# Attention and feed-forward kernel: float32 scores in the first six blocks, one output buffer per token group, three new plan estimates

## The chip, the cores and the metric

The kernel runs on one core of a Trainium2 chip as one launch. The core has a matrix engine (PE, with its weight loads shown apart as PEld), a vector engine (DVE), a scalar engine (ACT), a third one (POOL) and a queue that issues transfers (SP). The metric is the time on the device in microseconds (us); lower is better.

## The reference

Attention over 4 batches, 8 heads, 768 positions and 64 channels, then a feed-forward layer over the 3072 tokens that it gives.

```python
scores = scale * np.matmul(q, k.transpose(0, 1, 3, 2))
rel = pos[:, None] - pos[None, :]
is_global = pos[None, :] < int(n_global)          # 8 keys
is_local = (rel >= 0) & (rel < int(n_local))      # 96 keys
keep = is_global | is_local
dist = np.where(is_global & ~is_local, float(n_local), np.abs(rel))
scores = np.where(keep, scores - slopes * dist, -1000000000.0)
a = np.exp(scores - max); a = a / (sum + 1e-09)
x = matmul(a, v)                                  # (B, H, S, D) -> (B*S, H*D)
h = x @ w_in                                      # 512 -> 2048
g = h * (1.0 / (1.0 + np.exp(-h)))
return (g @ w_out).astype(np.float32)             # 2048 -> 512
```

## The kernel before, in words

**Tiling.** The 24 blocks (4 batches by 6) hold 128 tokens each; a block has 4 head pairs. A block looks at 128 keys if it is the first of its batch (NJ = 6 blocks per batch) and at 232 otherwise: 96 of the block before, 8 global ones and its own 128. Two blocks are a group for the feed-forward layer (12 groups of 256 tokens, 16 chunks f of the hidden width).

**A head pair's way.** PE turns keys and queries (`turn`, L448), ACT copies the high parts out of the PSUM bank (`high`, L503), and in blocks 0 to 5 DVE subtracts them to get the low parts (`low`, L507); both are float32r tiles, KH, KL, QH and QL. POOL carries the last 96 and the global keys over from the block before (`carry`, L514 and L516). `scores` (L528) adds three products, QH by KH, QH by KL and QL by KH, each for the two heads of the pair on partitions 0 to 63 and 64 to 127: six matmuls. DVE adds the bias and takes the extreme (L545), ACT takes the exponential (L553), PE turns the result (L578), ACT moves it to SBUF (L584), PE multiplies by the values (`values_q`, L612, in blocks 0 to 5, operands float32). After the fourth pair DVE divides the whole block (L628, tile xq), PE turns it back (L634), ACT and DVE make xh and xl (L643, L646). Blocks 6 to 23 use another form, with both parts stacked over the 128 partitions (`stack_scores`, L500; values at L598); the change leaves it as it is.

**Feed-forward.** `moe_h` (L763) takes 12 matmuls a chunk, `moe_o` (L788) 6. Groups 0 and 1 run side by side, since the weights come in one chunk after another: SP loads them, DVE puts each together from 64-bit words in three steps (L368, L374, L380), ACT makes the high part (L387), DVE the low part (L391). `moe_end` writes a group's two output tiles (`osb`), and `moe_out` sends each.

**What sets the order.** Nothing is ordered at run time. A planner (`Plan.run`) simulates the engines with costs in ns written at each `op(...)`, lets each engine take the ready operation of the lowest rank, and writes down the order; the engines then run their lists in that order and wait by semaphores. The estimate of a transfer is PAR["DL"] = 1900. Where the plan has PE without work before its time 60000 (PAR["WEND"]), it puts in a filler, a matmul of zeros that nothing reads (L899, tile wx), which keeps the engine at work. `big` is a pool of three buffers of 4 KB per partition: staged weights (w), R of the stacked blocks, weights that are read again for a check (c, L411), and the output tiles (osb) take turns in it.

```python
if best is None:
    if eng == "PE" and filler and t < fill_until and self.banks:
        order.append(lambda b=self.banks[-1]: filler(b))
```

Of the kernel before, what the change touches and what calls it, by code (L numbers as in the profile page):

```python
# [21 lines left out]
P = 128  # L22
# [5 lines left out]
FAR = 1.0e9  # L28
PAR = dict(

    LAT=140, SD=125, DL=1900, MG=60, T2=45000, LAT2=230, MG2=400, F0=600, F1=1200, C1=900, C2=3400, COLD=7000, WEND=60000,

    CAP=dict(po=4, av=2, s=4, h=3, tp=2, tq=4), HU=13,

# [136 lines left out]
def attn_moe(ctx, tc, q, k, v, n_global, n_local, w_in, w_out, out):  # L171
# [8 lines left out]
    NB = 2  # L180
# [213 lines left out]
    for n in range(2 * NFC):  # L394
        rank = PAR["C0"] + PAR["CR"] * n
        a, m, x = [] if lent(n) is not None else [Buf("big")], Buf("mid"), lent(n)
        o = op("DMA", 1456, rank - PAR["LW"], (lambda n=n: stage(n, "w")), [o_l[x]] if not a else (), a, PAR["DL"])
        o = op("DVE", 335, rank, (lambda n=n: conv1(n)), [o], [*a, m])
        o = op("DVE", 602, rank, (lambda n=n: conv2(n)), [o], [*a, m])
        o = op("DVE", 602, rank, (lambda n=n: conv3(n)), [o], [*a, m])  # L400
        if x is not None:
            o_l[x] = o
        o_wf = o
        hi = op("ACT", 520, rank, (lambda n=n: conv_hi(n)), [o] + (o_l if n >= 2 * NFC - 4 else []), [m])
        lo = op("DVE", 602, rank, (lambda n=n: conv_lo(n)), [hi], [m])
        o_w.append((hi, lo))
# [38 lines left out]
    def turn(i, nm, tp, p0=0, p1=NHP):  # L445
        blk[i]["t", nm, p0] = ps = bank(tp, NHP, P)
        for hp in range(p0, p1):
            nc.tensor.transpose(ps[:, hp], blk[i][nm][:, 2 * hp:2 * hp + 2, :], ident)  # L448

    def part(i, x):  # L450
        if x not in blk[i]:
            blk[i][x] = sb2.tile([P, NHP, WIN if x[0] == "K" else P], F32R, name=x)
        return blk[i][x][:, :, C1:] if x[0] == "K" else blk[i][x]


# [46 lines left out]
    def high(i, nm, p0=0, p1=NHP):  # L502
        nc.scalar.copy(part(i, nm.upper() + "H")[:, p0:p1], blk[i]["t", nm, p0][:, p0:p1])  # L503

    def low(i, nm, p0=0, p1=NHP):
        hi, lo = (part(i, nm.upper() + x)[:, p0:p1] for x in "HL")
        nc.vector.tensor_sub(lo, blk[i]["t", nm, p0][:, p0:p1], hi.bitcast(F32))  # L507

    def carry(i, x, glob):
        part(i, x)  # L510
        new, old = blk[i][x], blk[i - 1][x].bitcast(F32)
# [9 lines left out]
    def scores(i, hp, s):  # L521
        t = blk[i]
        w0, n = cols(i)
        t["s", hp] = ps = [bank(x, WIN) for x in s]
        for m, (x, y) in enumerate((("QH", "KH"), ("QH", "KL"), ("QL", "KH"))):
            for a in range(2):
                r = slice(a * D, (a + 1) * D)
                nc.tensor.matmul(  # L528
                    ps[a][:, :n], t[x][r, hp], t[y][r, hp, w0:], start=m == 0, stop=m == 2
                )  # L530

    def top_of(i, hp, a):
        t = blk[i]
# [120 lines left out]
    for i in range(B * NJ):  # L654
# [3 lines left out]
        if not i:  # L658
            xn = dict(k=Buf("qkn"), q=Buf("qkn"))
            for p0 in (0, NHP // 2):  # L660
                for nm in "kq":
                    p1, tp = p0 + NHP // 2, Buf("tq")
                    hi, lo = kk[nm.upper() + "H"], kk[nm.upper() + "L"]
                    o = op("DMA", 728, rank - lr, (lambda nm=nm, a=2 * p0, b=2 * p1: load(0, nm, a, b)), (), [xn[nm]], PAR["DL"])
                    o = op("PE", 220, rank, (lambda nm=nm, tp=tp, a=p0, b=p1: turn(0, nm, tp, a, b)), [o], [xn[nm], tp, hi, lo])
                    ob[nm + "h", p0] = o = op("ACT", 264, rank, (lambda nm=nm, a=p0, b=p1: high(0, nm, a, b)), [o], [tp, hi])
                    ob[nm + "l", p0] = op("DVE", 331, rank, (lambda nm=nm, a=p0, b=p1: low(0, nm, a, b)), [o], [tp, hi, lo])
        for nm in "kq" if i else "":
            xn, tp = Buf("qkn"), Buf("tq")
            hi, lo = kk[nm.upper() + "H"], kk[nm.upper() + "L"]  # L670
            o = op("DMA", 1456, rank - lr, (lambda i=i, nm=nm: load(i, nm)), (), [xn], PAR["DL"])
            o = op("PE", 440, rank, (lambda i=i, nm=nm, tp=tp: turn(i, nm, tp)), [o], [xn, tp, hi, lo])
            if i >= PAR["I0"]:
                hs = [op("ACT", 478, rank, (lambda i=i, nm=nm, a=a: stack_high(i, nm, a, False)), [o], [tp, x])
                      for a, x in enumerate((hi, lo))]
                for a, x in enumerate((hi, lo)):
                    y = x if nm == "k" else kk["R"]
                    ob[nm, a] = op("DVE", 602, rank, (lambda i=i, nm=nm, a=a: stack_low(i, nm, a)),
                                   hs + ([o_wf] if nm == "q" else []), [tp, x, y])
                    if nm == "q":  # L680
                        ob[nm, a, 2] = op(
                            "ACT", 520, rank + PAR["RQ"], (lambda i=i, a=a: twin_low(i, a)), [ob[nm, a]], [y]
                        )
                        ob[nm, a, 1] = op(
                            PAR["QS"], dict(ACT=520, POOL=1930, DVE=335)[PAR["QS"]], rank + PAR["RQ"],
                            (lambda i=i, nm=nm, a=a: stack_high(i, nm, a, True)), [hs[a]], [x]
                        )
                continue
            ob[nm + "h"] = op("ACT", 478, rank, (lambda i=i, nm=nm: high(i, nm)), [o], [tp, hi])
            ob[nm + "l"] = op("DVE", 602, rank, (lambda i=i, nm=nm: low(i, nm)), [ob[nm + "h"]], [tp, hi, lo])  # L690
        if j:
            old = o_k[i - 1]
            stacked = i >= PAR["I0"]
            for x, y in ((("KH", ("k", 0)), ("KL", ("k", 1))) if stacked else (("KH", "kh"), ("KL", "kl"))):
                for gl, cost in ((True, 227), (False, 1400)):
                    ob[x, gl] = op(
                        "POOL", cost, rank, (lambda i=i, x=x, gl=gl: carry(i, x, gl)),
                        [*(old[z] for z in (((y, 0), (y, NHP // 2)) if i == 1 else (y,))), old.get((x, True)), ob[y]],
                        [kb[i - 1][x], kk[x]],
                    )  # L700
# [5 lines left out]
        for hp in range(NHP):  # L706
            u = NHP * i + hp
            stacked = i >= PAR["I0"]
            s, pe, pt, tp = [Buf("s") for _ in range(1 if stacked else 2)], Buf("pe"), Buf("pt"), Buf("tp")
            ks = [kk[x] for x in ("KH", "KL", "QH", "QL") + (("R",) if stacked else ())]  # L710
# [23 lines left out]
            before["move"] = o_m[-1]  # L734
            pts.append(pt)
            if not plain:
                last = op("PE", 460 if j else 230, u - PAR["RV"], (lambda i=i, hp=hp, av=pav: values_q(i, hp, av)),
                          [o_m.pop(), last] + o_v, [pt, pav, kk["vn"]] + ([kk["vp"]] if j else []))
            elif not stacked or hp == NHP - 1:
                last = op("PE", ((1860 if j else 980) if stacked else 540 if j else 290), u - PAR["RV"],  # L740
                          (lambda i=i, hp=hp, av=pav: values_of(i, hp, av)),
                          [*o_m, last] + o_v, [*pts, pav, xb[g]["xh"], xb[g]["xl"], kk["vn"]] + ([kk["vp"]] if j else []))
                o_m, pts = [], []
# [46 lines left out]
            )  # L790

    def moe_end(g, tt, half=None):
        if ("out", g, tt) not in mo:
            mo["out", g, tt] = sb3.tile([P, DM], F32, name="osb", tag="big")
        h = slice(0, DM) if half is None else slice(half * DM // 2, (half + 1) * DM // 2)
        o, po = mo["out", g, tt][:, h], mo["po", g, tt][:, h]
        if tt % 2 and not half:
            nc.scalar.mul(o, po, 0.5)
        else:
            nc.vector.tensor_scalar(o, po, 0.5, None, ALU.mult)  # L800

    def moe_out(g, tt, half=None):
        n = g * NB + tt
        h = slice(0, DM) if half is None else slice(half * DM // 2, (half + 1) * DM // 2)
        eng = nc.scalar if half == 0 else nc.sync
        eng.dma_start(out[n * P:(n + 1) * P, h], mo["out", g, tt][:, h])

    o_h = {}
    FIRST = -1e6
    for g in range(NGRP):  # L810
# [3 lines left out]
        for f in range(NFC):  # L814
# [260 lines left out]
```

## Time and profile before

| | |
|---|---|
| median of 3 runs | 734.85 us (733.05 to 736.74) |
| the profiled execution | 735.96 us |
| its span, first to last instruction | 734.2 us |
| PE busy | 722.7 us (98%), 5236 matmuls |
| DVE, ACT, POOL busy | 471.3, 422.0, 28.1 us |
| mean granted PE clock | 0.996 |

The busy time of PE is a union of matmuls whose ends are modelled, so they overlap; what a matmul takes from the engine is read from the distance between the starts of neighbours. The span falls into four stretches: a start of some 8 us; the attention of blocks 0 to 3 up to some 60 us; feed-forward groups 0 and 1 up to some 153 us, with the remaining heads of blocks 4 and 5 and the first of block 6 up to some 167 us; and from there ten groups of the same pattern to the end.

### The profile page before, as it was taken

Reading aid. Unit: us, or ns where it says so; the run is one execution under the profiler, and the core shown is the slowest. Engines: PE = TensorE matmul, PEld = TensorE weight load, DVE = VectorE, ACT = ScalarE, POOL = GpSimd, SP = SyncE. Lnnn points to the kernel's source line nnn. Section 1 sums busy time; section 2 is a strip of 40 time slices with the busy share of each in tenths; the row PEclk is TensorE's granted clock in tenths of the full one; section 3 lists DMA queues with packets and bytes.
Section 4 is the critical chain, followed back from the end, with each engine's and each line's share of the span. In section 5 each row is a group of like instructions: output and inputs, shape, how many; then the busy total and the mean of one; then the engine's idle time right before and its main releaser. Section 6 shows DMA issues by size and latency. Waiting matters only on the chain.

```text
span 734.2 us, 14157 instructions
## 1 busy us (share of the span) xinstructions
PE 722.7 (98%) x5236; PEld 650.9 (89%) x5236; DVE 471.3 (64%) x1417; ACT 422.0 (57%) x1105; POOL 28.1 (4%) x91
## 2 busy tenths in 40 slices
PE   8999999999999999999999999999999999999996
PEld 6889988988999999898999999999899999998995
DVE  4689999986567566666665665765666756544322
ACT  5887544477566466565665665755756756543321
POOL 2010000000000000000000000000000000000000
PEclk9999999999999999999999999999999999999999
DMA  7587553424033242241340421512412312000001
GB/s 153 137 255 194 166 172 107 152 82 115 26 105 87 55 112 68 74 113 45 87 111 16 128 73 41 142 53 61 130 44 70 103 54 56 30 1 1 29 0 34
DMA packets 117500, 63.97 MB, mean 87 GB/s; under 512 B 93744, under 2 KB 110384, under 8 KB 117424
## 3 DMA queue, kind: packets, MB, share of 16 engines
q1 hardware_dynamic: 116992, 62.86, 31.6%
q8 instruction: 43, 0.70, 0.4%
q14 instruction: 33, 0.27, 0.1%
q10 hardware_dynamic: 432, 0.13, 0.1%
HBM read 56.69 MB, written 6.29 MB: 86 GB/s over the span
## 4 chain that ended last, share of the span: by engine, by line
PE 97%; DMA 1%; DVE 1%; issue 0%; SPq 0%; ACT 0%; DVEq 0%
PE bank L763 38%; PE bank L788 36%; PE bank L578 5%; PE bank L598 4%; PE bank L500 4%; PE bank L448 3%; PE bank L612 3%; PE bank L528 2%; PE bank L899 1%; DMA qn<-in_q_dram 1%; DMA out_dram<-osb 1%; PE bank L634 0%; DVE osb L800 0%; DVE R L487 0%; DVE pe L569 0%
## 5 line engine op out<-in xcount | busy, mean ns | idle before, releaser
L763 PE MATMUL bank<-xh,WIH 128*128 128x256 f32 x768 | 224.6, 292 | 0.8 <-ACT xh L643 0.8
L763 PE MATMUL bank<-xl,WIH 128*128 128x256 f32 x768 | 217.0, 283 | 0.7 <-DVE xl L646 0.7
L763 PE MATMUL bank<-xh,WIL 128*128 128x256 f32 x768 | 215.6, 281 | 0.0
L763 PEld LDWEIGHTS bank<-xh,WIH 128*128 128x128 f32 x768 | 145.2, 189 | 10.0 <-issue 2.2
L763 PEld LDWEIGHTS bank<-xl,WIH 128*128 128x128 f32 x768 | 145.4, 189 | 7.3 <-DVE xl L646 0.9
L763 PEld LDWEIGHTS bank<-xh,WIL 128*128 128x128 f32 x768 | 145.6, 190 | 0.0
L788 PE MATMUL bank<-WOH,gh 128*128 128x512 f32 x336 | 136.1, 405 | 0.0
L769 ACT ACTIVATE th<-bank 128x256 f32<-128x256 f32 x192 | 73.6, 383 | 106.6 <-PE bank L763 104.6
L788 PE MATMUL bank<-WOH,gl 128*128 128x512 f32 x336 | 132.4, 394 | 0.0
L788 PE MATMUL bank<-WOL,gh 128*128 128x512 f32 x336 | 131.9, 393 | 0.0
L777 ACT CAST gh<-th 128x256 fp32r<-128x256 f32 x192 | 77.4, 403 | 91.9 <-PE bank L788 62.4
L773 DVE SCALAR_TENSOR_TENSOR th<-th,bank 128x256 f32<-128x256 f32 x192 | 80.4, 419 | 64.8 <-ACT th L769 63.3
L781 DVE TENSOR_TENSOR gl<-th,gh 128x256 fp32r<-128x256 f32 x192 | 81.5, 424 | 50.7 <-ACT gh L777 48.6
L545 DVE CUSTOM_DVE_ANT_0 pe<-bank,B 128x232 f32<-128x232 f32 (+1 forms) x192 | 69.0, 376 | 63.2 <-PE bank L500 57.2
L553 ACT ACTIVATE pe<-pe,NM 128x232 f32<-128x232 f32 (+1 forms) x192 | 90.3, 471 | 18.6 <-DVE NM L545 16.4
L584 ACT COPY pt<-bank 128x512 f32<-128x512 f32 (+1 forms) x96 | 52.6, 549 | 52.5 <-PE bank L578 52.3
L788 PEld LDWEIGHTS bank<-WOH,gl 128*128 128x128 f32 x336 | 63.0, 188 | 15.1
L788 PEld LDWEIGHTS bank<-WOH,gh 128*128 128x128 f32 x336 | 63.4, 189 | 6.7 <-issue 0.3
L788 PEld LDWEIGHTS bank<-WOL,gh 128*128 128x128 f32 x336 | 63.4, 189 | 6.4
L578 PE MATMUL bank<-ident,pe 128*128 128x128 f32 (+1 forms) x352 | 55.0, 275 | 0.1
L578 PEld LDWEIGHTS bank<-ident,pe 128*128 128x128 f32 (+1 forms) x352 | 42.0, 137 | 6.6 <-DVE pe L569 0.6
L411 DVE TENSOR_REDUCE TOP<-c 128x1 f32<-128x512 int16 x64 | 42.3, 681 | 3.2 <-DMA c<-in_moe_w_in_dram 3.2
(119 smaller groups left out, 939.1 us busy)
## 6 DMA issues: line engine op xcount, KB each, us to landing
c<-in_moe_w_in_dram SPq DMA_DIRECT2D x16, 512.0 KB, 4.0
c<-in_moe_w_out_dram SPq DMA_DIRECT2D x16, 512.0 KB, 4.4
vn<-in_v_dram SPq DMA_DIRECT2D x24, 256.0 KB, 3.4
w<-in_moe_w_in_dram SPq DMA_DIRECT2D x12, 512.0 KB, 3.8
w<-in_moe_w_out_dram SPq DMA_DIRECT2D x12, 512.0 KB, 3.6
kn<-in_k_dram SPq DMA_DIRECT2D x23, 256.0 KB, 3.0
qn<-in_q_dram SPq DMA_DIRECT2D x23, 256.0 KB, 3.1
out_dram<-osb SPq DMA_DIRECT2D x23, 256.0 KB, 3.0
```

The source lines that it names most:

```text
L411: nc.vector.tensor_reduce(TOP[:, i, n:n + 1], top, AX.X, (ALU.min, ALU.max)[i], apply_absolute_value=True)
L500: nc.tensor.matmul(ps[:, a, :n], t[x][:, hp], t[K[a]][:, hp, w0:], start=not m, stop=m == 1)
L545: nc.vector.tensor_tensor_reduce(t["p", hp][:, a, :n], t["s", hp][a][:, :n], B1[:, h] if i % NJ else B0[:, h], -SC, 3.0e38, ALU.add, ALU.m ...
L553: nc.scalar.activation(x, x, AF.Exp, bias=NM[:, i * H + h:i * H + h + 1], scale=-1.0, accum_out=t["sum", hp][:, a:a + 1],)
L578: nc.tensor.transpose(ps[:n, c, a], pe[:, a, c0:c0 + n], ident)
L584: nc.scalar.copy(t["pt", hp][:, c], t["tp", hp][:, c])
L763: nc.tensor.matmul(ph, w[:, c, fs], x[:, c], start=not c and not n, stop=c == NCC - 1 and n == 2)
L769: nc.scalar.activation(th, mo["ph", g, f], AF.Tanh, scale=0.5)
L773: nc.vector.scalar_tensor_tensor(gf, gf, 1.0, mo["ph", g, f], ALU.add, ALU.mult)
L777: nc.scalar.copy(gh, mo["th", g, f])
L781: nc.vector.tensor_sub(gl, mo["th", g, f], mo["gh", g, f].bitcast(F32))
L788: nc.tensor.matmul(po, a[:, s], w_o(w, f), start=f == 0 and n == 0, stop=f == NFC - 1 and n == 2)
```

## The change

1. `part` makes the key and query tiles of blocks 0 to 5 float32 (names KHw and QHw). `low`, KL and QL are gone there. `scores` is one float32 product for each of the two heads: two matmuls in the program instead of six.
2. `carry` moves only the high tile in blocks 1 to 5; the plan's costs of a carry go from 227 and 1400 to 155 and 455.
3. The plan's cost of `values_q` goes from 460 to 900 (230 to 450 in a batch's first block). The cost of scores stays 640. (The third cost that the diff changes, in the branch of `values_of`, is not used: IV = I0 = 6.)
4. The plan's estimate for a weight transfer is 2900 and for an output transfer 3400, both 1900 before.
5. A group's two output tiles are one tile of 4 KB in one `big` buffer.

```diff
@@ PAR
-    LAT=140, SD=125, DL=1900, MG=60, ...
+    LAT=140, SD=125, DL=1900, DW=2900, DO=3400, MG=60, ...
@@ weights
-        o = op("DMA", 1456, rank - PAR["LW"], (lambda n=n: stage(n, "w")), [o_l[x]] if not a else (), a, PAR["DL"])
+        o = op("DMA", 1456, rank - PAR["LW"], (lambda n=n: stage(n, "w")), [o_l[x]] if not a else (), a, PAR["DW"])
@@ part
+    def whole(i):
+        return i < PAR["I0"]
+
     def part(i, x):
         if x not in blk[i]:
-            blk[i][x] = sb2.tile([P, NHP, WIN if x[0] == "K" else P], F32R, name=x)
+            f = whole(i)
+            blk[i][x] = sb2.tile(
+                [P, NHP, WIN if x[0] == "K" else P], F32 if f else F32R, name=x + "w" * f, tag=x
+            )
@@ low, carry, scores
-    def low(i, nm, p0=0, p1=NHP):
-        hi, lo = (part(i, nm.upper() + x)[:, p0:p1] for x in "HL")
-        nc.vector.tensor_sub(lo, blk[i]["t", nm, p0][:, p0:p1], hi.bitcast(F32))
...
-        for m, (x, y) in enumerate((("QH", "KH"), ("QH", "KL"), ("QL", "KH"))):
-            for a in range(2):
-                r = slice(a * D, (a + 1) * D)
-                nc.tensor.matmul(
-                    ps[a][:, :n], t[x][r, hp], t[y][r, hp, w0:], start=m == 0, stop=m == 2
-                )
+        for a in range(2):
+            r = slice(a * D, (a + 1) * D)
+            nc.tensor.matmul(ps[a][:, :n], t["QH"][r, hp], t["KH"][r, hp, w0:], start=True, stop=True)
@@ the operations of a block
-                    ob[nm + "l", p0] = op("DVE", 331, rank, (lambda nm=nm, a=p0, b=p1: low(0, nm, a, b)), [o], [tp, hi, lo])
-            ob[nm + "l"] = op("DVE", 602, rank, (lambda i=i, nm=nm: low(i, nm)), [ob[nm + "h"]], [tp, hi, lo])
-            for x, y in ((("KH", ("k", 0)), ("KL", ("k", 1))) if stacked else (("KH", "kh"), ("KL", "kl"))):
-                for gl, cost in ((True, 227), (False, 1400)):
+            for x, y in ((("KH", ("k", 0)), ("KL", ("k", 1))) if stacked else (("KH", "kh"),)):
+                for gl, cost in ((True, 155), (False, 455)):
-                last = op("PE", 460 if j else 230, u - PAR["RV"], (lambda i=i, hp=hp, av=pav: values_q(i, hp, av)),
+                last = op("PE", 900 if j else 450, u - PAR["RV"], (lambda i=i, hp=hp, av=pav: values_q(i, hp, av)),
@@ output
-        if ("out", g, tt) not in mo:
-            mo["out", g, tt] = sb3.tile([P, DM], F32, name="osb", tag="big")
+        if ("out", g) not in mo:
+            mo["out", g] = sb3.tile([P, NB, DM], F32, name="osb", tag="big")
...
+        ob = Buf("big")
         for tt in range(NB):
-            ob = Buf("big")
...
-                op("DMA", 728, FIRST + rank, (lambda g=g, tt=tt, h=h: moe_out(g, tt, h)), [o], [ob], PAR["DL"])
+                op("DMA", 728, FIRST + rank, (lambda g=g, tt=tt, h=h: moe_out(g, tt, h)), [o], [ob], PAR["DO"])
```

Since the plan is made anew, the order changes too, up to the start of group 2; from there on all engines have the same order as before. PE's list holds 74 fillers before and 28 after, ten of them at its very start in both; 144 score matmuls before and 48 after. DVE's list loses the 14 subtractions of `low`, POOL's ten carries.

**Place 1: PE at the start**, from the turning of the second half of block 0's keys (kn) on; qn are the queries, KH, KL, QH and QL the split tiles, KHw and QHw the float32 ones, wx the filler's zeros. Before:

```order
L448 MATMUL bank_84<-ident,kn 128x128 x2
L899 LDWEIGHTS wx
L899 MATMUL bank_82<-wx 128x256
L448 MATMUL bank_85<-ident,qn 128x128 x2
L528 MATMUL bank_86<-KH,QH 128x128
L528 MATMUL bank_87<-KH,QH 128x128
L528 MATMUL bank_86<-KL,QH 128x128
L528 MATMUL bank_87<-KL,QH 128x128
L528 MATMUL bank_86<-KH,QL 128x128
L528 MATMUL bank_87<-KH,QL 128x128
```

and now:

```order
L448 MATMUL bank_84<-ident,kn 128x128 x2
L532 MATMUL bank_85<-KHw,QHw 128x128
L532 MATMUL bank_86<-KHw,QHw 128x128
L448 MATMUL bank_87<-ident,qn 128x128 x2
L532 MATMUL bank_88<-KHw,QHw 128x128
L532 MATMUL bank_89<-KHw,QHw 128x128
L899 LDWEIGHTS wx
L899 MATMUL bank_84<-wx 128x256
```

The six matmuls of a pair became two, and the first pair now stands ahead of the second half of the queries.

**Place 2: PE behind the turning back of block 0** (xq), where the turned exponentials (pe) of block 1 follow. Before:

```order
L634 MATMUL bank_87<-ident,xq 128x128 x4
L578 MATMUL bank_89<-ident,pe 104x128 x2
L578 MATMUL bank_89<-ident,pe 128x128 x2
L899 LDWEIGHTS wx
L899 MATMUL bank_86<-wx 128x256
L899 LDWEIGHTS wx
L899 MATMUL bank_86<-wx 128x256
```

and now (vp and vn are the values, pt the exponentials moved to SBUF):

```order
L636 MATMUL bank_88<-ident,xq 128x128 x4
L448 MATMUL bank_85<-ident,kn 128x128 x4
L614 MATMUL bank_82<-vp,pt 128x64
L614 MATMUL bank_82<-vn,pt 128x64
L614 MATMUL bank_82<-vp,pt 128x64
L614 MATMUL bank_82<-vn,pt 128x64
L580 MATMUL bank_89<-ident,pe 104x128 x2
```

Five fillers stood there; now the next keys and a values product, which the plan counts twice as long as it did, take the place.

**Place 3: PE where block 5 ends and group 2 begins**, from the last turned exponentials ahead of xq to the first matmul of group 2 (xh, WIH). Before:

```order
L578 MATMUL bank_89<-ident,pe 128x128 x2
L612 MATMUL bank_87<-vp,pt 128x64
L612 MATMUL bank_87<-vn,pt 128x64
L612 MATMUL bank_87<-vp,pt 128x64
L612 MATMUL bank_87<-vn,pt 128x64
L448 MATMUL bank_83<-ident,qn 128x128 x4
L634 MATMUL bank_86<-ident,xq 128x128 x4
L578 MATMUL bank_82<-ident,pe 128x128 x2
L578 MATMUL bank_85<-ident,pe 128x128 x2
L763 MATMUL bank_88<-xh,WIH 128x256
```

and now, where the values product of block 5 is the row just ahead of the first one shown:

```order
L580 MATMUL bank_86<-ident,pe 128x128 x2
L788 MATMUL bank_82<-w_last_1599,gh 128x512
L788 MATMUL bank_82<-w_last_1600,gh 128x512
L788 MATMUL bank_82<-w_last_1599,gl 128x512
L788 MATMUL bank_87<-w_last_1599,gh 128x512
L788 MATMUL bank_87<-w_last_1600,gh 128x512
L788 MATMUL bank_87<-w_last_1599,gl 128x512
L580 MATMUL bank_83<-ident,pe 128x128 x2
L636 MATMUL bank_88<-ident,xq 128x128 x4
L448 MATMUL bank_84<-ident,qn 128x128 x4
L580 MATMUL bank_86<-ident,pe 128x128 x2
L763 MATMUL bank_85<-xh,WIH 128x256
```

Six matmuls of the output product of groups 0 and 1 now stand between the last values product and xq, and the queries of block 7 moved behind xq.

## Rows read from the trace of the kernel before

**Rows 1.** The profile's first part: busy us, share of the span, count.

```profile
PE 722.7 (98%) x5236; PEld 650.9 (89%) x5236; DVE 471.3 (64%) x1417; ACT 422.0 (57%) x1105; POOL 28.1 (4%) x91
```

**Rows 2.** Whom PE waited for in the whole span: us, times, longest.

```profile
...
PE bank L763 <- ACT xh L643: 0.8, 1, 0.8
...
PE bank L634 <- DVE xq L628: 0.7, 1, 0.7
PE bank L763 <- DVE xl L646: 0.7, 1, 0.7
...
```

**Rows 3.** Busy us (instructions) of PE, PEld, DVE, ACT, POOL by stretch; clock, DMA.

```profile
20.00:60.00 40.00, 40.00 (x360) 35.69 (x360) 31.53 (x102) 31.87 (x94) 4.00 (x12) 1.00 0.76 205
100.00:150.00 50.00, 50.00 (x318) 45.02 (x318) 48.40 (x103) 23.94 (x53) 0.00 (x0) 1.00 0.42 127
165.00:170.00 5.00, 3.52 (x16) 3.07 (x17) 2.26 (x4) 3.83 (x9) 0.00 (x0) 0.78 0.67 125
170.00:175.00 5.00, 5.00 (x37) 4.82 (x36) 2.79 (x11) 2.88 (x10) 1.26 (x4) 0.88 0.00 1
```

**Rows 4.** PE in time (start, us, line): a pair's scores and the values behind.

```profile
24.47 0.37 PE L528 MATMUL bank<-KH,QH 64*128 64x232 f32 x2
24.68 0.27 PE L528 MATMUL bank<-KL,QH 64*128 64x232 f32 x2
24.79 0.27 PE L528 MATMUL bank<-KH,QL 64*128 64x232 f32 x2
25.00 0.43 PE L612 MATMUL bank<-vp,pt 104*128 104x64 f32 x2
25.27 0.39 PE L612 MATMUL bank<-vn,pt 128*128 128x64 f32 x2
25.49 0.39 PE L612 MATMUL bank<-vp,pt 104*128 104x64 f32 x2
...
```

**Rows 5.** PE in time, block 0: scores, fillers, turned keys, and fillers later.

```profile
8.82 0.41 PE L528 MATMUL bank<-KL,QH 64*128 64x128 f32 x2
9.03 0.41 PE L528 MATMUL bank<-KH,QL 64*128 64x128 f32 x2
9.38 1.25 PE L899 MATMUL bank<-wx 128*128 128x256 bf16 x5
10.42 1.06 PE L448 MATMUL bank<-ident,kn 128*128 128x128 f32 x4
...
17.63 0.71 PE L899 MATMUL bank<-wx 128*128 128x256 bf16 x5
18.18 0.38 PE L578 MATMUL bank<-ident,pe 128*128 128x128 f32 x2
```

**Rows 6.** PE in time: float32 values of a stacked block, four matmuls a row.

```profile
206.13 0.39 PE L598 MATMUL bank<-pt,vp 104*64 104x128 f32 x4
206.35 0.39 PE L598 MATMUL bank<-pt,vn 128*64 128x128 f32 x4
```

**Rows 7.** Groups by line and form: busy us, mean ns, idle before.

```profile
L899 PE MATMUL bank<-wx 128*128 128x256 bf16 x74 | 14.0, 324 | 1.1 <-DVE wx L307 1.1
...
L507 DVE TENSOR_TENSOR KL<-bank,KH 128x512 fp32r<-128x512 f32 x5 | 3.4, 682 | 0.0
...
L507 DVE TENSOR_TENSOR KL<-bank,KH 128x256 fp32r<-128x256 f32 x2 | 0.8, 424 | 3.3 <-ACT KH L503 3.3
```

**Rows 8.** All engines in time where block 5 ends; releaser of a wait in brackets.

```profile
166.36 0.39 PE L763 MATMUL bank<-xh,WIH 128*128 128x256 f32 x1 [0.78 <-ACT xh L643]
...
167.39 0.39 PE L763 MATMUL bank<-xl,WIH 128*128 128x256 f32 x1 [0.65 <-DVE xl L646]
```

**Rows 9.** DVE and PE in time: a wait for values; a weight and its first user.

```profile
32.46 0.69 DVE L628 TENSOR_TENSOR xq<-bank,sums 128x512 f32<-128x512 f32 x1 [2.42 <-PE bank L612]
...
147.01 0.69 DVE L391 TENSOR_TENSOR WIL<-wf,WIH 128x512 fp32r<-128x512 f32 x1
...
148.57 0.28 PE L763 MATMUL bank<-xh,WIH 128*128 128x256 f32 x1
```

More of the change, by code (lines that the diff above doesn't have):

```diff
@@ L29 @@
 PAR = dict(
-    LAT=140, SD=125, DL=1900, MG=60, T2=45000, LAT2=230, MG2=400, F0=600, F1=1200, C1=900, C2=3400, COLD=7000, WEND=60000,
+    LAT=140, SD=125, DL=1900, DW=2900, DO=3400, MG=60, T2=45000, LAT2=230, MG2=400, F0=600, F1=1200, C1=900, C2=3400, COLD=7000, WEND=60000,
     CAP=dict(po=4, av=2, s=4, h=3, tp=2, tq=4), HU=13,
@@ L503, in high @@
         nc.scalar.copy(part(i, nm.upper() + "H")[:, p0:p1], blk[i]["t", nm, p0][:, p0:p1])
-    def low(i, nm, p0=0, p1=NHP):
-        hi, lo = (part(i, nm.upper() + x)[:, p0:p1] for x in "HL")
-        nc.vector.tensor_sub(lo, blk[i]["t", nm, p0][:, p0:p1], hi.bitcast(F32))
     def carry(i, x, glob):
         part(i, x)
-        new, old = blk[i][x], blk[i - 1][x].bitcast(F32)
+        new, old = blk[i][x], blk[i - 1][x]
+        old = old if whole(i) else old.bitcast(F32)
         if glob:
@@ L662, in attn_moe @@
                     p1, tp = p0 + NHP // 2, Buf("tq")
-                    hi, lo = kk[nm.upper() + "H"], kk[nm.upper() + "L"]
+                    hi = kk[nm.upper() + "H"]
                     o = op("DMA", 728, rank - lr, (lambda nm=nm, a=2 * p0, b=2 * p1: load(0, nm, a, b)), (), [xn[nm]], PAR["DL"])
-                    o = op("PE", 220, rank, (lambda nm=nm, tp=tp, a=p0, b=p1: turn(0, nm, tp, a, b)), [o], [xn[nm], tp, hi, lo])
-                    ob[nm + "h", p0] = o = op("ACT", 264, rank, (lambda nm=nm, a=p0, b=p1: high(0, nm, a, b)), [o], [tp, hi])
-                    ob[nm + "l", p0] = op("DVE", 331, rank, (lambda nm=nm, a=p0, b=p1: low(0, nm, a, b)), [o], [tp, hi, lo])
+                    o = op("PE", 220, rank, (lambda nm=nm, tp=tp, a=p0, b=p1: turn(0, nm, tp, a, b)), [o], [xn[nm], tp, hi])
+                    ob[nm + "h", p0] = op("ACT", 264, rank, (lambda nm=nm, a=p0, b=p1: high(0, nm, a, b)), [o], [tp, hi])
         for nm in "kq" if i else "":
@@ L671, in attn_moe @@
             o = op("DMA", 1456, rank - lr, (lambda i=i, nm=nm: load(i, nm)), (), [xn], PAR["DL"])
-            o = op("PE", 440, rank, (lambda i=i, nm=nm, tp=tp: turn(i, nm, tp)), [o], [xn, tp, hi, lo])
+            o = op("PE", 440, rank, (lambda i=i, nm=nm, tp=tp: turn(i, nm, tp)), [o], [xn, tp, hi] if whole(i) else [xn, tp, hi, lo])
             if i >= PAR["I0"]:
@@ L709, in attn_moe @@
             s, pe, pt, tp = [Buf("s") for _ in range(1 if stacked else 2)], Buf("pe"), Buf("pt"), Buf("tp")
-            ks = [kk[x] for x in ("KH", "KL", "QH", "QL") + (("R",) if stacked else ())]
+            ks = [kk[x] for x in (("KH", "KL", "QH", "QL") if stacked else ("KH", "QH")) + (("R",) if stacked else ())]
             n = cols(i)[1]
@@ L736, in attn_moe @@
             if not plain:
-                last = op("PE", 460 if j else 230, u - PAR["RV"], (lambda i=i, hp=hp, av=pav: values_q(i, hp, av)),
+                last = op("PE", 900 if j else 450, u - PAR["RV"], (lambda i=i, hp=hp, av=pav: values_q(i, hp, av)),
                           [o_m.pop(), last] + o_v, [pt, pav, kk["vn"]] + ([kk["vp"]] if j else []))
             elif not stacked or hp == NHP - 1:
-                last = op("PE", ((1860 if j else 980) if stacked else 540 if j else 290), u - PAR["RV"],
+                last = op("PE", ((1860 if j else 980) if stacked else 726 if j else 508), u - PAR["RV"],
                           (lambda i=i, hp=hp, av=pav: values_of(i, hp, av)),
@@ L792, in moe_end @@
     def moe_end(g, tt, half=None):
-        if ("out", g, tt) not in mo:
-            mo["out", g, tt] = sb3.tile([P, DM], F32, name="osb", tag="big")
+        if ("out", g) not in mo:
+            mo["out", g] = sb3.tile([P, NB, DM], F32, name="osb", tag="big")
         h = slice(0, DM) if half is None else slice(half * DM // 2, (half + 1) * DM // 2)
-        o, po = mo["out", g, tt][:, h], mo["po", g, tt][:, h]
+        o, po = mo["out", g][:, tt, h], mo["po", g, tt][:, h]
         if tt % 2 and not half:
@@ L805, in moe_out @@
         eng = nc.scalar if half == 0 else nc.sync
-        eng.dma_start(out[n * P:(n + 1) * P, h], mo["out", g, tt][:, h])
+        eng.dma_start(out[n * P:(n + 1) * P, h], mo["out", g][:, tt, h])
     o_h = {}
```

## The prediction

> **What bounds the kernel now.** I read the busy times first. PE is busy 98% of the span [rows 1], but that share is a union of overlapping, modelled ends, so I next looked at whom PE waits for [rows 2]: 0.8, 0.7 and 0.7 us stand out of a span of 734.2. The table of stretches shows PE without a gap in 20 to 60 and in 100 to 150 us and a hole only in 165 to 170 [rows 3]. So the time is the sum of what stands in PE's list, and the change can win in three ways: by taking matmuls out, by filling the hole, or by having PE at its higher clock for longer.
>
> Two things qualify this. Part of the list is filler: 74 matmuls of zeros [rows 7], which PE runs because the plan believed that nothing was ready. And other engines run close behind: DVE is busy 48.4 of 50 us in 100 to 150, ACT 31.87 of 40 in 20 to 60 [rows 3]. Work taken from PE shortens the time only as far as these two keep up.
>
> **(a) Fillers, 74 to 28.** Ten open the list in both kernels, where PE waits for the first data anyway. The other 64 become 18. PE starts at 1.2 GHz: in block 0 five fillers of 256 columns take 9.38 to 10.42, 0.21 us each; at 17.63 five take 0.55 us, 0.11 each, which is 2.4 GHz [rows 5]. In the order, the half-rate start loses 5 of 16 and the rest 41 of 48: 5 x 0.21 + 41 x 0.108 = 1.0 + 4.4 = **-5.4 us**, if nothing waits in their place. They stood there because the plan counts a values product at 460 ns. The trace has its eight instructions 0.11 apart (25.00, 25.27, 25.49 for successive pairs, the first one's start included [rows 4]), 0.88 us in all. So PE ran later than planned, and at run time others waited for it: DVE 2.42 us before dividing a block [rows 9]. With 900 the plan is near the truth and has fewer holes to fill.
>
> **(b) Scores, 24 head pairs.** In blocks 1 to 5 a pair's three products run from 24.47 to 25.00 [rows 4]: 0.53 us, which I read as three pairs of matmuls at 0.11 and 0.10 each to get in and out. The float32 form does not occur here with 64 partitions and 232 columns. The nearest row is the values product of the stacked blocks: float32 too, two heads side by side, two instructions each; four instructions of 128 columns take 0.22 us (206.13 to 206.35 [rows 6]), hence 0.11 for one pass of both heads. With 232 columns a pass is 0.11 x 232/128 = 0.20, two are 0.40, with 0.20 for getting in and out 0.60: +0.07 a pair, x 20 = +1.4. In block 0 (128 columns, half rate) a pass of a pair takes 0.21 (8.82 to 9.03 [rows 5]); two for three: -0.21 x 4 = -0.85. Net **+0.6 us**. Lower bound: a pass as quick as the present ones, 0.22 + 0.20 = 0.42, -0.11 x 20 - 0.85 = -3. Upper bound: the two heads one after the other, rival B.
>
> What [rows 4] show is one pass over 232 columns in 0.11 us for the present type. On this the Trainium skill speaks against the change: "FP8 and Floating Point Precision", section TensorE Precision Notes, gives true FP32 four passes through the array. Four passes at 0.11 for three would make a pair 0.64 instead of 0.53 and, by this estimate, the sum 0.8 us later than mine. Rows 6 agree in kind: 0.22 us for 128 columns is about four times what one column per cycle at 2.4 GHz would take.
>
> **(c) DVE and POOL.** DVE loses 14 subtractions; the rows of KL are five of 0.68 and two of 0.42 us [rows 7], those of QL as many: 10 x 0.682 + 4 x 0.424 = 8.5 us. POOL loses ten carries of its 28.1 us [rows 1]. Nothing of this is on PE's path, so I cost it at **0**; but it decides whether the 4.4 us of (a) can be kept. The last weight is ready on DVE at 147.01 + 0.69 = 147.70, its first user starts at 148.57 [rows 9]: a lead of 0.9 us, with DVE full. A PE that is 4 us quicker would run into DVE there; with 8.5 us less ahead of that weight DVE stays ahead. Its new order of work moves nothing else past this point.
>
> **(d) The end of block 5.** PE is idle there for 0.7 (xq), 0.78 (xh) and 0.65 us (xl) [rows 2, 8], 2.2 in all, and a stretch at the lower clock follows: the granted clock is 0.78 in 165 to 170 and 0.88 in 170 to 175 [rows 3]. Of the second, 12% of 5 us at half rate cost 0.6 us; 165 to 170 has 22%, 1.1 us: 1.7 together. (Place 3) Six output matmuls, some 1.4 us, now stand between the last values product and xq, so they cover the wait for DVE's division, and the queries of block 7 behind xq cover part of the wait for xh. I leave 0.65 for xl, and half a chance of the slow stretch: -1.5 - 0.85 = **-2.4 us**. Bounds: 0 (the holes move along) and -3.9.
>
> **(e) Waits in place of fillers.** A filler is a place where the plan had nothing to do. At run time a part of those becomes real waiting, above all for ACT, which has 40 - 31.87 = 8.1 us to spare in 20 to 60 [rows 3] and keeps all its work: its spare is larger than the 4.4 us, but the plan's order cannot use all of it. **+1.5 us**; bounds 0 and 4.4, all of the full-rate fillers.
>
> **(f) The start.** PE leaves the lower clock at about 17.6 us, after a stretch of values products and fillers [rows 5]. Fewer fillers can move that moment either way; each us of it costs or gives half a us. I take **0**, bounds -3 and +6.
>
> **(g) Transfer estimates and the shared output buffer.** Longer estimates move loads earlier or their users later in the plan. From group 2 on every engine's order is the same as before, and PE has no wait on an output buffer among those of [rows 2]; **0**. If the shared buffer came free late, DVE's next output would wait, while PE has a chunk of other work; at worst some tenths of a us a group.
>
> **Sum.** -5.4 + 0.6 + 0 - 2.4 + 1.5 + 0 + 0 = -5.7. Against the profiled execution, 735.96 us (span 734.2, 1.8 around it), that is 730.3. That execution lies 1.1 above the median of 734.85, so the forecast is 734.85 - 5.7 = **729.2 us**.
>
> **Rivals** (on the median's scale).
> B, the heads do not run side by side. Matmuls of 64 partitions run in pairs today, one of each head in a step of 0.11 us [rows 4], but the only float32 pairs seen have another arrangement, heads on different columns [rows 6]. One after the other, a pair costs 4 x 0.20 + 0.20 = 1.00, +0.47 x 20 = +9.4, block 0 + 0.85: +10.3 for +0.6, so 729.2 + 9.7 = 738.9; PE then again covers the waits of (e), -1.5: **737.4, slower**. It decides from 0.53 + 5.7/20, about 0.8 us a pair; a pair in the changed trace tells at once. For it: no row shows this form. Against it: the present type on the same partitions. Chance 0.13. The Trainium skill's "TensorEngine Tiling (Array Packing)" lets different tiles execute matmuls in parallel and speaks against B; no float32 row here shows that for 64 partitions.
> C, the clock. Fillers hold PE at work; with 46 fewer the low clock lasts to some 30 us instead of 17.6: 12.4 x 0.5 = +6, **735.2**. For it: the rise came amid fillers, and the fall at the end of block 5 came after a hole of 2.2 us [rows 3, 8]. Against: 11 of 16 remain in this stretch and the removed ones give way to real work. Chance 0.14.
> E, ACT becomes the bound and takes back all of the 4.4: +2.9 more, **732.1**, within 0.5%. For it: 80% busy [rows 3], and ACT is in every head pair's chain. Chance 0.13.
> D, more than forecast: scores at their lower bound (-3.6 more) or no new waits and no slow stretch (-2.4 more), **722 to 726**. Chance 0.10.
> That the change does not do what it says is excluded: matmuls, subtractions and fillers are gone from the lists.
>
> **How the numbers follow.** My forecast, 726 to 731.2, has 0.50. A measurement of this kernel can tell about 0.5% from no change, so the bounds are 731.2 and 738.5. Faster: 0.50 + D 0.10 = 0.60. Same: E, most of C and B, 0.13 + 0.12 + 0.09 = 0.34. Slower: the rest of B and C, 0.06. The range goes from 724.0, inside D, to 736.5, which takes in E, C and some of B's lesser forms; about 2 in 10 stay outside.
>
> **What would show it.** Right: a float32 pair at 0.60 us from its first matmul to the next operation; fillers 28, those after 20 us some 7; PE still dense in 20 to 60; DVE's busy time down by 8.5 us with the last weight several us ahead of its first user; waits at the end of block 5 under 1 us, then a granted clock above 0.95 in the 5 us around it; from group 2 on the same distances as before. Wrong: a pair at 1.0 us (B); 0.21 us between matmuls of 256 columns well after 18 us (C); PE waiting for ACT's exponentials or turned copies for 4 us in 20 to 60 (E); new waits on DVE between 100 and 150 us, which would say that the weights, not PE, set the pace after all.

## The result, and the profile after

| | before | after |
|---|---|---|
| median of 4 runs | 734.58 us (733.05 to 736.74) | 726.80 us (726.21 to 728.07) |
| ratio | | 0.9894, 95% interval 0.9866 to 0.9923 |
| profiled execution, its span | 735.96, 734.2 us | 726.68, 724.9 us |

Five more rounds later, with eight of the first ten fillers writing to other banks, gave 0.9877 (0.9861 to 0.9894), with medians of 736.06 and 726.74 us. The change is faster by 1.1 to 1.2%.

The page's first part after, which answers [rows 1]:

```profile
PE 715.0 (99%) x5142; PEld 640.5 (88%) x5142; DVE 463.5 (64%) x1403; ACT 420.6 (58%) x1105; POOL 24.9 (3%) x81
```

Whom PE waited for after (us in all, times, longest), the answer to [rows 2]:

```profile
PE bank L580 <- DVE pe L571: 0.6, 1, 0.6
...
PE bank L763 <- DVE xl L648: 0.3, 1, 0.3
```

The stretches after, in the columns of [rows 3]:

```profile
20.00:60.00 40.00, 40.00 (x329) 34.55 (x330) 32.88 (x110) 35.41 (x105) 2.03 (x6) 1.00 0.93 249
...
100.00:150.00 50.00, 50.00 (x322) 43.96 (x321) 41.03 (x93) 23.79 (x58) 0.21 (x2) 1.00 0.33 100
...
165.00:170.00 5.00, 5.00 (x40) 4.32 (x40) 4.39 (x12) 2.89 (x8) 0.00 (x0) 1.00 0.25 59
170.00:175.00 5.00, 5.00 (x40) 4.39 (x37) 4.65 (x14) 4.76 (x12) 0.00 (x0) 1.00 0.70 166
```

PE has no gap in 20 to 60 us although ACT is now busy 35.41 of 40 there (31.87 before); DVE has room in 100 to 150 (41.03 of 50, 48.40 before); and the granted clock no longer falls.

PE in time after (start, us, line): two lone score pairs of block 0, two pairs in a row and a lone one of block 1, and the end of block 5:

```profile
7.26 0.80 PE L532 MATMUL bank<-KHw,QHw 64*128 64x128 f32 x4
7.99 0.69 PE L448 MATMUL bank<-ident,qn 128*128 128x128 f32 x2
8.61 0.80 PE L532 MATMUL bank<-KHw,QHw 64*128 64x128 f32 x4
9.34 1.25 PE L899 MATMUL bank<-wx 128*128 128x256 bf16 x5
...
17.03 1.05 PE L532 MATMUL bank<-KHw,QHw 64*128 64x232 f32 x8
18.02 0.66 PE L614 MATMUL bank<-vn,pt 128*128 128x64 f32 x4
...
23.80 0.66 PE L532 MATMUL bank<-KHw,QHw 64*128 64x232 f32 x4
24.39 0.66 PE L448 MATMUL bank<-ident,qn 128*128 128x128 f32 x4
...
157.96 0.60 PE L448 MATMUL bank<-ident,qn 128*128 128x128 f32 x4
159.18 0.43 PE L580 MATMUL bank<-ident,pe 128*128 128x128 f32 x2 [0.63 <-DVE pe L571]
159.38 0.36 PE L763 MATMUL bank<-xh,WIH 128*128 128x256 f32 x1
160.01 0.39 PE L763 MATMUL bank<-xl,WIH 128*128 128x256 f32 x1 [0.27 <-DVE xl L648]
```

A float32 pair takes 24.39 - 23.80 = 0.59 us by itself, two in a row 18.02 - 17.03 = 0.99: 0.40 a pair and 0.20 for getting in and out, once for a row of pairs. In block 0 a lone pair takes 7.99 - 7.26 = 0.73 at half rate. At the end of block 5 0.90 us of waits are left of 2.2 [rows 2, 8]: 0.27 for xl, and 0.63 in a new place, for exponentials.

**Where the 9.3 us between the two profiled executions went.** I summed, for each kind of matmul on PE, the distances from its start to the next start, up to the first matmul of group 2:

| | before | after | difference |
|---|---|---|---|
| fillers (74, 28), the first ten among them | 13.12 us | 7.19 us | -5.93 |
| score matmuls of blocks 0 to 5 (144, 96 instructions in the trace) | 13.50 | 14.41 | +0.91 |
| waits where block 5 ends (2.17, 0.90) | | | -1.27 |
| stretch at the lower clock behind it (3.4 us long, 0) | | | -1.7 |
| rise of the clock at the start (at 17.6, at 14.8 us) | | | -1.4 |

Together -9.4, against 726.68 - 735.96 = -9.28. (The first two rows hold a little of the last one's, since the earlier rise also shortens some fillers and the first pairs of block 1; so the close match is partly chance.) The medians of these four runs differ by 7.8, since the profiled execution of before was 1.4 above its median; those of the later, more numerous runs differ by 9.3.

### The profile page after: what moved, and what is told of

The parts are those of the page before. It is cut to its first block, busy times and chain, and to the rows that moved or that the text cites. A ratio compares the mean times of both kernels' runs of the same rounds, so it can differ in the third digit from the quotient of the medians.

```text
span 724.9 us, 13945 instructions
## 1 busy us (share of the span) xinstructions
PE 715.0 (99%) x5142; PEld 640.5 (88%) x5142; DVE 463.5 (64%) x1403; ACT 420.6 (58%) x1105; POOL 24.9 (3%) x81
## 4 chain that ended last, share of the span: by engine, by line
PE 97%; DVE 1%; DMA 1%; ACT 1%; issue 0%; SPq 0%; ACTq 0%
PE bank L763 38%; PE bank L788 37%; PE bank L580 5%; PE bank L600 4%; PE bank L508 4%; PE bank L448 3%; PE bank L614 3%; PE bank L532 2%; DMA qn<-in_q_dram 1%; PE bank L899 0%; PE bank L636 0%; ACT pe L555 0%; DVE osb L800 0%; ACT osb L798 0%; DVE xl L648 0%
```

## The experiments

Each was run beside the kernel before, in five rounds; ratios are to it. The experiments were run in three groups of four, in which the kernel before had medians of 736.11, 735.94 and 736.06 us. In all but the first and the one that fills the hole, eight of the first ten fillers also write to other banks, which the edits below leave out; the change itself, run with only that, is among them.

**Only the fillers at the higher clock taken out, order as before.**

```diff
     def filler(b):
+        fills.append(b)
+        if len(fills) > 26:
+            return
         nc.tensor.matmul(bank(b, 2 * P), warm[:, :P], warm, start=True, stop=True)
```

> The kernel before in its own order, but of its 74 fillers only the first 26 are emitted: the 48 that ran at the higher clock (5.7 us between their starts in the trace) are left out, nothing else changes. Theory (the fillers were pure cost, since PE ran later than planned): 734.6 - 5.7 and up to 1.5 of new waits, 729 to 730.5. Rival (DVE sets the pace: the last weight is ready 0.9 us before its first user, so a quicker PE runs into it): PE waits for DVE between 100 and 150 us and all but some 1 to 1.5 us come back, 733 to 734.

Measured: 731.80 us, 0.9941 (0.9922 to 0.9961): -4.3 us of 5.7. The stretch of 20 to 60 us and PE's waits:

```profile
20.00:60.00 40.00, 38.41 (x332) 33.77 (x331) 33.07 (x104) 32.52 (x96) 4.96 (x12) 1.00 0.82 215
```

```profile
PE bank L634 <- DVE xq L628: 1.0, 3, 0.3
...
PE bank L578 <- ACT pe L553: 0.6, 2, 0.4
```

Of the 40 us PE now waits 1.6, for the division of a block and for exponentials. There is no wait for a weight: the last one of the first product (WIL) is ready at 145.04 us in this trace, its user starts at 145.92, the lead of 0.9 as in [rows 9], because DVE itself moved 2.7 us ahead. The waits and the lower clock at the end of block 5 stay as they were. The rival is wrong: DVE's weights do not set the pace; they follow PE, which in attention DVE waits for.

**Only the plan's cost of a values product, in the kernel before.**

```diff
-                last = op("PE", 460 if j else 230, u - PAR["RV"], (lambda i=i, hp=hp, av=pav: values_q(i, hp, av)),
+                last = op("PE", 900 if j else 450, u - PAR["RV"], (lambda i=i, hp=hp, av=pav: values_q(i, hp, av)),
```

> The kernel before with one number changed, the plan's cost of a values product (900 and 450 for 460 and 230): 34 fillers for 74, scores in three products and DVE's subtractions stay. (Eight of the first ten fillers write to different banks, so that each bank is written before it is read.) Theory (the plan's estimate carries most of the gain): 40 fewer fillers, -4.4 to -5, so 729.5 to 730.5. Rival (without DVE's relief the shorter list runs into the weights): 733 or more, with waits of PE for DVE in 100 to 150 us.

Measured: 728.25 us, 0.9895 (0.9877 to 0.9914), -7.9 us where -4.4 to -5 was expected. One number gives all that the whole change gives. It does better than the run above, which took out more fillers. Its trace shows three reasons: the new order fills the places (PE busy in 39.91 of 40 us in 20 to 60), its wait at the end of block 5 is 1.1 us in one piece, and the granted clock does not fall behind it. A fourth lies in this execution, the quickest of its six (726.81 us): its step changes at 11.5 us instead of 17.6, worth some 3 us (last section). DVE still does its 14 subtractions, and yet the last weight of the first product, ready at 132.46, has its first user at 138.62: a lead of 6.2 us.

```profile
20.00:60.00 40.00, 39.91 (x360) 35.64 (x359) 37.88 (x117) 35.31 (x104) 4.46 (x12) 1.00 0.94 255
...
165.00:170.00 5.00, 5.00 (x45) 4.38 (x44) 3.04 (x7) 3.22 (x7) 0.00 (x0) 1.00 0.67 194
```

```profile
PE bank L578 <- DVE pe L569: 1.1, 1, 1.1
```

```profile
131.77 0.69 DVE L391 TENSOR_TENSOR WIL<-wf,WIH 128x512 fp32r<-128x512 f32 x1
...
138.62 0.28 PE L763 MATMUL bank<-xh,WIH 128*128 128x256 f32 x1
```

**The changed kernel with that cost put back** (the two lines above the other way round).

> The changed kernel with only the plan's cost of a values product put back (460 and 230): 52 fillers for 28, float32 scores stay. Theory: 24 more fillers at 0.11 us, +2.6: 729 to 730. Rival (the float32 scores and DVE's relief carry the gain, whatever the plan believes): within 0.7 us of 726.8.

Measured: 733.09 us, 0.9957 (0.9941 to 0.9973). Both expectations miss: it loses more than its 24 fillers, some 6 us of the change's 9 (0.9957 against 0.9877). Fillers cost 9.76 us here for 7.19 in the change, +2.6 as expected; the rest is the end of block 5, where the waits of before are back and the stretch at the lower clock with them, in this execution at twice its price (22% and 46% of 5 us, 1.1 + 2.3 = 3.4 us against 1.7):

```profile
PE bank L763 <- ACT xh L645: 0.8, 1, 0.8
PE bank L763 <- DVE xl L648: 0.7, 1, 0.7
...
PE bank L636 <- DVE xq L630: 0.4, 1, 0.4
```

```profile
160.00:165.00 5.00, 3.12 (x15) 2.31 (x14) 3.36 (x10) 4.73 (x10) 0.00 (x0) 0.78 1.13 251
165.00:170.00 5.00, 5.00 (x27) 5.00 (x26) 1.73 (x7) 1.71 (x6) 0.27 (x2) 0.54 0.35 100
```

So the better order at the end of block 5, too, comes from the values estimate.

**The 14 subtractions put back on DVE in the changed kernel.**

```diff
+                    op("DVE", 331, rank, (lambda nm=nm, a=p0, b=p1: low(0, nm, a, b)), [o], [tp, hi, kk[nm.upper() + "L"]])
...
+            op("DVE", 602, rank, (lambda i=i, nm=nm: low(i, nm)), [ob[nm + "h"]], [tp, hi, lo])
```

> The changed kernel with the 14 subtractions of low put back on DVE, planned as before, their results read by nobody: 8.5 us more work of DVE in the first 70 us, PE's list nearly the same (29 fillers). Theory (DVE is off the path by some us): 726.8 to 728. Rival (the relief is what lets PE keep its gain): the last weights come late, PE waits for DVE between 100 and 150 us, 730 to 733.

Measured: 724.89 us, 0.9848 (0.9829 to 0.9868). Useless work on DVE made it no slower; beside the change's own 0.9877 it is if anything quicker, quicker than either expectation. Its last weight of the first product is ready at 134.94 + 0.69 = 135.63 and used at 141.10, 5.5 us later, as in the change (132.33 and 137.79). What differs is the order that the plan found: PE's list of waits ends, in this kernel, with the transfers of the start, and nothing waits at the end of block 5. So this run does not weigh the subtractions alone: it says that DVE has room for them.

```profile
PE bank L913 <- DVE wx L307: 1.1, 1, 1.1
PE bank L448 <- DMA qn<-in_q_dram: 0.9, 1, 0.9
PE bank L448 <- DMA kn<-in_k_dram: 0.6, 1, 0.6
```

**Everything but the float32 scores**: the kernel before with the three estimates and the shared output tile.

```diff
-    LAT=140, SD=125, DL=1900, MG=60, ...
+    LAT=140, SD=125, DL=1900, DW=2900, DO=3400, MG=60, ...
-                last = op("PE", 460 if j else 230, ...
+                last = op("PE", 900 if j else 450, ...
-            mo["out", g, tt] = sb3.tile([P, DM], F32, name="osb", tag="big")
+            mo["out", g] = sb3.tile([P, NB, DM], F32, name="osb", tag="big")
```

> The changed kernel without its first two points: scores of blocks 0 to 5 in three products, 14 subtractions and all carries as before, but the three new plan estimates and the shared output tile. Theory (after the run with the values estimate alone: the plan carries the gain, float32 scores and the relief of DVE and POOL are worth nothing): ratio to the kernel before 0.988 to 0.991. Rival (float32 scores are worth the 0.43% that they gave under the old estimates): 0.993 to 0.995.

Measured: 727.73 us, 0.9881 (0.9868 to 0.9894), the same as the whole change (0.9877). The float32 scores, with the relief of DVE and POOL, are worth nothing that these runs can tell. Under the old values estimate the rest of the change together gave 0.43% (the third run); under the new one its first two points add nothing.

**The transfer estimates and the output tile undone in the changed kernel**, together and the estimates alone.

```diff
-    LAT=140, SD=125, DL=1900, DW=2900, DO=3400, MG=60, ...
+    LAT=140, SD=125, DL=1900, DW=1900, DO=1900, MG=60, ...
...
-            mo["out", g] = sb3.tile([P, NB, DM], F32, name="osb", tag="big")
+            mo["out", g, tt] = sb3.tile([P, DM], F32, name="osb", tag="big")
```

> The changed kernel with both transfer estimates back at 1900 and two output tiles per group again. Theory (these parts are worth 0): 0.987 to 0.992 of the kernel before. Rival (loads planned too late make PE wait, or the buffers tie transfers to each other): 0.994 or more, with new waits on transfers in the trace.

> The changed kernel itself, with nothing altered but that eight of the first ten fillers write to different banks, as in the runs it is to be compared with. All theories: 0.987 to 0.991 of the kernel before. It says whether the runs with the subtractions put back (0.985) and with old transfer estimates and two output tiles (0.985) are really quicker than the change (then 0.987 or more here) or whether the wide interval of the first comparison hid that the change is as quick (0.985 here).

> The changed kernel with the two transfer estimates back at 1900, the shared output tile kept. Theory (the place where block 5 ends decides: with these estimates other work covers its waits): no wait of PE over 0.3 us in 150 to 165 us and a ratio of 0.984 to 0.987. Rival (the gain of the run with both undone came from the output tiles): the waits stay and the ratio is that of the change, 0.988 to 0.990.

Measured: both undone 725.40 us, 0.9851 (0.9837 to 0.9865); the estimates alone 725.93 us, 0.9866 (0.9848 to 0.9885); the change itself 726.74 us, 0.9877 (0.9861 to 0.9894). Both undone is quicker than the first expectation (0.987 to 0.992). The two kernels with the old estimates have the same list on PE from its first matmul to its last, so the output tile changes nothing there, and PE has no wait behind the start in either; in the change's copy the waits of 0.6 and 0.3 us at the end of block 5 stand as in the change (shown above).

The intervals touch, so a loss of some 1 us by the new transfer estimates is likely, and not settled. A gain by them, or a tie between the transfers by the shared tile, shows nowhere.

**The hole at the end of block 5 filled, in the kernel before.**

```diff
+        for _ in range(6 if i == 5 else 0):
+            nc.tensor.matmul(bank(tp, 2 * P), warm[:, :P], warm, start=True, stop=True)
         for hp in range(NHP):
             nc.tensor.transpose(ps[:, hp], t["xq"][:, 2 * hp:2 * hp + 2, :], ident)
...
+        for _ in range(12 if (g, f, c) == (2, 0, 0) else 0):
+            nc.tensor.matmul(ph, warm[:, :P], warm, start=True, stop=True)
```

> The kernel before with 18 more fillers where block 5 ends: 6 ahead of the turning back of xq, 12 ahead of the first matmul of group 2, in time in which PE waited; nothing else changes. Theory (the hole of 2.2 us brings the fall of the clock): granted clock 1.00 through 160 to 175 us, the waits there gone from PE's list of waits, -1.4 to -1.9 us, ratio 0.9974 to 0.998. Rival (the fall comes from something else, or fillers do not hold the clock): the half-rate stretch stays and the ratio is 1.000 to 1.001.

Measured: 734.45 us, 0.9975 (0.9962 to 0.9988), -1.8 us by the ratio (0.9 to 2.8) and -1.5 by the medians. With zeros in the hole the granted clock stays; of the waits 0.3 us (xl) and 0.2 (exponentials) are left, where the expectation had none:

```profile
165.00:170.00 5.00, 4.65 (x41) 4.35 (x39) 2.39 (x5) 4.04 (x10) 0.00 (x0) 1.00 0.63 111
170.00:175.00 5.00, 5.00 (x35) 4.59 (x35) 3.89 (x15) 3.43 (x11) 1.26 (x4) 1.00 0.44 116
```

The matmuls do no useful work, so nearly all of the 1.8 is the price of the lower clock, which the rows of before put at 1.7: this half of (d) is shown by itself. The same kind of instruction costs 0.11 us where PE is dense, and eighteen of them give back some 1.8 where it would stand still.

**Fillers of the start**, in two ways: the plan takes PE to be at half rate until 12000, and the change's order with only the first ten fillers.

```diff
-    ... COLD=7000, WEND=60000,
+    ... COLD=12000, WEND=60000,
```

> The changed kernel with one number of the plan changed: it takes PE to run at half rate until 12000 instead of 7000 (the traces so far show the rise at 11.5 to 18.0 us). 17 fillers for 28. Theory (a plan nearer to the trace puts in fewer fillers, each pure cost): 11 fewer, most of them at 0.21 us, -1.5 to -2: ratio to the kernel before 0.986 to 0.988. Rival (fillers of the start hold PE at work until the clock has risen): the rise comes later than 18 us and the ratio is 0.990 or more.

> The changed kernel in its own order, with only the first ten fillers emitted: the other 18, of which 8 ran at half rate (0.21 us each) and 10 at the full one (0.11), are left out. Theory (pure cost): -2.8 us and up to 1.5 of new waits, ratio 0.985 to 0.987 when the change itself is 0.989. Rival (the fillers of the start keep PE at work until the clock rises; without them it rises later): rise in the trace later than 18 us, ratio 0.989 or more.

Measured: COLD=12000 727.76 us, 0.9895 (0.9882 to 0.9907); ten fillers 724.82 us, 0.9852 (0.9836 to 0.9867). With ten fillers the rival is wrong: the clock is up at 12.0 us, and 1.9 us are won against the change's copy. PE in time at that place; the lone pair takes 0.73 us still, as at half rate above, but the four turning matmuls behind it take 12.40 - 11.85 = 0.55, where four such matmuls stand in [rows 5] at 10.42 with 1.06 us as their length, 0.71 here:

```profile
11.12 0.80 PE L532 MATMUL bank<-KHw,QHw 64*128 64x128 f32 x4
11.85 0.71 PE L448 MATMUL bank<-ident,qn 128*128 128x128 f32 x4
12.40 0.56 PE L614 MATMUL bank<-vn,pt 128*128 128x64 f32 x4
```

The run with COLD=12000 stays open; neither expectation holds. It has 11 fillers fewer and no wait at the end of block 5, and won nothing by the median. Its profiled execution was the fastest of its five (725.41): its span of 723.5 us is 1.4 below the change's, although the rise came at 16.9 us, 2.1 later than there. What its other executions did is in no trace.

**The best of these without its last fillers**: old transfer estimates, two output tiles, 21 of 27 fillers.

> The run with old transfer estimates and two output tiles per group, now without its 6 fillers at the higher clock (21 of 27 emitted, order unchanged): 0.66 us less on PE. Theory (fillers at the higher clock are pure cost, those of the start are kept): ratio 0.984 to 0.9855. Rival (waits come in their place): 0.985 to 0.987, no gain.

Measured: 724.44 us, 0.9847 (0.9833 to 0.9860), the quickest kernel of the study, if hardly to be told from the run with all its fillers (0.9851).

## Why the prediction was right, and where it was not

The time of 729.2 us was forecast, 726.8 measured, inside the range; faster with 1.1% where 0.8% was forecast. The gain was put too low: 5.7 us, against 7.8 here and 9.3 in the later runs. The sum came out near the truth, partly for other reasons than the ones given, and partly by luck (f).

- **(a)** -5.4 forecast, -5.9 measured, and the cause of most of it is shown: with only the values estimate changed, the kernel before loses 40 of the 46 fillers and reaches 0.9895.
- **(b)** A pair in blocks 1 to 5 takes 0.59 us, 0.60 was forecast; two passes of 0.196 us and 0.20 of getting in and out. Rival B is wrong: the heads' float32 products run side by side. Mis-sized is block 0: -0.85 forecast, about 0 measured. Before, two pairs stood in a row and shared the getting in and out (7.90 to 9.38 us, 0.74 each); now each stands alone and takes 0.73. I had counted passes and left out that the order tears the pairs apart. Blocks 1 to 5 came out at +0.9 for +1.4, since there the new order puts four of the 20 pairs into two rows of two, which saves 0.2 each. In all +0.9 for +0.6. The Trainium skill's four passes ("FP8 and Floating Point Precision", TensorE Precision Notes) agree with the trace: two instructions of 0.196 us for 232 columns are four times 0.098, about one column per cycle at 2.4 GHz. My estimate from that page, 0.64 a pair, was too long because it took a present step of 0.11 for each pass.
- **(c)** The step that failed. I let DVE's relief decide whether the gain of (a) can be kept. The subtractions put back cost nothing that shows (0.9848, in an order of its own), and the kernel before with the right values estimate keeps the whole gain with all 14 of them: its lead is 6.2 us without any relief. (What I called the last weight is the last of the first product; the last of the output product is made 3 to 4 us later.) A lead of 0.9 us in the old trace meant that DVE follows PE, not that it holds PE up.
- **(d)** -2.4 forecast, -3.0 measured: 0.90 us of waits left instead of 0.65, most of it in a place that I had not named (0.63 for exponentials, 0.27 for xl), and the slow stretch gone altogether, where I had put half a chance. Filling the hole in the old kernel shows the price, 1.8 us.
- **(e)** +1.5 forecast, 0 in the change. Taking the fillers out of the old order does bring 1.6 us of waits; the new order does not have them, since the right estimate moves ready work there. Rival E is wrong: ACT is busier than I feared, 35.41 of 40 us, and PE does not wait.
- **(f)** 0 forecast; the profiled pair shows -1.4. Most of that may be chance: four kernels (the change's copy, both runs with the old transfer estimates, and the one with 21 fillers) have the same PE list up to 20 us, with the same banks, and change their step at 12.8, 13.1, 14.6 and 16.9 us, the change itself at 14.8. With the old list three traces have 17.1, 17.6 and 18.0, but the kernel before with the values estimate alone, whose list is the same up to 14.4 us, has 11.5. Whether the change has a part in it is not settled. A part of the medians' difference may hide here, at most some 3 us. Rival C, that the loss of fillers keeps the clock low, is wrong for this order (rise at 12.0 us with only ten).
- **(g)** 0 forecast; the runs lean to a loss of about 1 us by the transfer estimates, not settled.

Rival D's 722 to 726 was just not reached by the change, and reached by five of its variants (724.4 to 725.9). Yet its second form, no new waits and no slow stretch, is what happened: 2.4 us below the forecast is 729.2 - 2.4 = 726.8, the time measured, and I had set D's upper end at 726 against its own sum. Its first form, scores at their lower bound, is wrong (a pair at 0.59 us, not 0.42).

## What to carry to other kernels

Where a planner sets the order, hold each of its costs beside the trace first: one estimate at half of the measured 0.88 us cost 1%, more than the arithmetic that was rewritten beside it. Split a change of several parts on the chip before believing any of them; here one number did it all, one part did nothing, and one leaned the other way. On an engine that bounds the time, fillers are cost in dense work and gain only in a hole that would bring its clock down, so put them there by place.

## What the hardware showed

The moment at which PE's step halves at the start is not fixed by PE's list: it lies between 11.5 and 18.0 us in the traces of this study. Two kernels whose PE lists are the same up to 20 us, the one with old transfer estimates and two output tiles, and the same with 21 of its 27 fillers, show it at 16.9 and at 12.8 us. First the one, then the other, at the same turned queries and the same three fillers:

```profile
13.41 1.12 PE L448 MATMUL bank<-ident,qn 128*128 128x128 f32 x4
15.49 0.85 PE L903 MATMUL bank<-wx 128*128 128x256 bf16 x3
```

```profile
13.17 0.66 PE L448 MATMUL bank<-ident,qn 128*128 128x128 f32 x4
14.29 0.49 PE L905 MATMUL bank<-wx 128*128 128x256 bf16 x3
```

The earliest is that of the kernel with the values estimate alone, whose list is the same up to there as the one of [rows 5] (only the banks of eight of the first fillers differ):

```profile
10.52 1.06 PE L448 MATMUL bank<-ident,kn 128*128 128x128 f32 x4
11.51 0.33 PE L528 MATMUL bank<-KH,QH 64*128 64x128 f32 x2
11.67 0.28 PE L528 MATMUL bank<-KL,QH 64*128 64x128 f32 x2
11.79 0.28 PE L528 MATMUL bank<-KH,QL 64*128 64x128 f32 x2
```

The steps of 0.11 us from 11.67 on are those of the higher clock; in the kernel before the same pairs were 0.21 apart. The column of the granted clock does not show this: it reads 1.00 in the kernel before in 10 to 15 us too, where the steps are 0.21, so at the start the level has to be read from the steps.

```profile
10.00:15.00 5.00, 5.00 (x29) 4.37 (x28) 2.73 (x18) 3.79 (x15) 3.09 (x10) 1.00 1.27 217
```

Each us of it is worth half a us: the two kernels with old transfer estimates, whose PE lists are the same throughout, rise at 16.9 and 14.6 us, and their spans are 725.0 and 723.7. So two profiles should be compared only after it is taken off; between 11.5 and 18.0 us it comes to 3 us. How much of the spread of untraced runs it makes is not shown: the five of the quickest kernel lie within 0.4 us, the six with the values estimate alone within 2.7.

The other surprise is the price of getting into and out of a row of score pairs, 0.10 us each way at 2.4 GHz and about 0.15 at 1.2 within the row, so that pairs in a row cost 0.40 and lone ones 0.59 us. The neighbours pay too: in the changed kernel the matmul ahead of a lone pair takes 0.20 us to the next start (23.59 to 23.80) and the one behind it 0.16 (24.39 to 24.55), where 0.11 is usual. I put it down to the change between matmuls of 128 and of 64 partitions, since it is there with one type on both sides (float32 turns and scores) and with different ones; no run tests this by itself.
